# Fewer warm-up matmuls, a shorter layer norm of tile 0 and re-ordered first loads in an MLP kernel on one core

## The chip, the cores and the metric

One core of a Trainium2 chip runs the whole program. The metric is the device time of one launch in microseconds (us), the median of several launches. The time is about 1.75 us longer than the span of the trace (first to last instruction), so the two are used side by side.

## The reference

```python
B, S, D, F = 1, 2048, 1024, 3584          # all inputs bf16
def reference(x, w1, b1, w2, b2):
    y = (x - mean(x)) / sqrt(var(x) + 1e-5)          # over the last axis
    h = gelu_tanh(y @ w1 + b1)
    return h @ w2 + b2
```

## The kernel before

Both products are done as 2x2 block products with seven products in place of eight. For that the normalised and transposed tiles y are combined on VectorE into **T sums** (T1 to T4), and w1 and w2 into sums of their own. The rows of x come in tiles of 128. Tiles 0 to 3 are transposed by TensorE and multiplied at once, in small "waves". Tiles 4 to 7 are transposed by DMA, and only when they have landed can the T sums be made. What I call **the join** is the point where TensorE, done with the products that need only y (the first 60 large matmuls), goes on to those that need T sums. What I call **the head** is all that TensorE does up to its first wave.

The kernel schedules itself. Each operation is a task with an engine, an estimated duration and the data that it reads and writes. A list scheduler fixes the order on each engine; a packer then gives every buffer its place in memory by a random search from a seed, and each shared place is one more dependency. A task's latest start (`alap`) follows from its users, or from a "due" time that is given by hand.

```python
# the scheduler: among the tasks that are READY, the one with the smallest alap is started
while q and q[0][0] <= now + 1e-9:            # q: waiting tasks, by the time at which they are ready
    _, _, t = heapq.heappop(q)
    heapq.heappush(heaps[e], (t.alap, t.i, t))
...
t.alap = fin - t.lat - t.dur * 1.3 - 0.1      # fin: the users' alap, or the due time if that is earlier

# the head
for ch in range((RH + 1) // 2):
    w1_load(0, ch, "A1")                      # two loads of 256 KB each; they depend on nothing
for i in range(4):
    pr.due = (None, HEAD_LN[i]); norm(i)      # x tile -> statistics -> rstd -> y
...
for bank in range(7):
    warm(1, bank=bank, full=True)             # 128x512 matmuls of ones, to wake the clock
warm(20)                                      # 128x128
for n, c in ((8, c_st[0][0]), (8, c_mv[0]), (6, c_rstd[0])):
    warm(n, c)                                # 8 more behind each stage of tile 0's norm
to_yT_pe(0, 0, (7, 6, 5, 4))                  # tile 0 through TensorE, in four pieces
...                                           # waves of tiles 0 to 3
# the join's other arm
def to_yT_dma(b, i):                          # tiles 4 to 7
    dma("SP", lambda e: e.dma_start_transpose(dst, v16(xbuf)), ...)
def tsum(b, t):                               # four sums of one tile, 128x512 each, on DVE
    T1 = B12 - B11;  T2 = B22 - T1;  T3 = B22 - B12;  T4 = B21 - T2
for i in range(4, 8):
    due(lambda: (to_yT_dma(0, i), tsum(0, i - 4)), HEAD_DUE[0] + HEAD_DUE[1] * (i - 4))()
```

(The body of `tsum` is put in short form; "..." are cuts.)

## Time and profile before

| | kernel before |
|---|---|
| time, median (range) | 333.39 us (333.37 to 333.67, 3 runs) |
| span of the profiled execution | 332.7 us, in a launch of **334.39 us** |
| TensorE, first warm-up / clock released / first wave | 1.07 / 7.02 / 8.63 us |
| TensorE at the join / wait there / long row of matmuls from | 30.21 / 0.4 / 30.61 us |
| VectorE busy | 90% |

The timeline of the kernel before shows the other arm of the join. The columns of the timeline are the start, the busy time, engine, line and operation, then the output, the inputs, the number of instructions, and in brackets the idle time ahead and what ended it.

```profile
18.98 5.93 SPq L733 DMA_TRANSPOSE mem<-mem  x3
24.51 1.54 DVE L751 TENSOR_TENSOR mem<-mem 128x512 f16<-128x512 f16 x4
25.88 1.23 SPq L733 DMA_TRANSPOSE mem<-mem  x1
26.56 4.66 DVE L751 TENSOR_TENSOR mem<-mem 128x512 f16<-128x512 f16 x12 [0.50 <-DMA mem<-mem]
30.61 1.69 PE L920 MATMUL ps<-mem 128*128 128x512 f16 x7 [0.40 <-DVE mem L751]
```

The four transposes are issued by SP from 18.98 us on. The first lands at 24.25 us and VectorE makes its four sums. The second lands at 26.54 us.

### The profile page before, as it was taken

What the parts mean: (1) busy time and instruction counts of PE and PEld (TensorE: products, weight loads), DVE (VectorE), ACT (ScalarE), POOL (GpSimd) and SP (SyncE); (2) the same over time, 40 slices, a digit from 0 to 9 for tenths busy, and PEclk for the clock granted to TensorE, in tenths of its full rate; (3) what the DMA queues carried; (4) which work ended last, traced back from release to release, by engine and by line L of the source; (5) the groups of instructions that cost most, each with busy time, mean ns of one, the idle gap of its engine ahead of it and who ended that gap; (6) DMA issues with size and microseconds to landing.
All of it is one profiled execution on the core that took longest, in us unless ns stands there. A gap on an engine that the chain in (4) does not pass through costs nothing.

```text
span 332.7 us, 4721 instructions
## 1 busy us (share of the span) xinstructions
PE 328.1 (99%) x1692; PEld 156.2 (47%) x1692; DVE 299.3 (90%) x488; ACT 181.8 (55%) x311; POOL 13.6 (4%) x29
## 2 busy tenths in 40 slices
PE   8999999999999999999999999999999999999996
PEld 6943444444444444444444444444444444444445
DVE  4988999998999949995899999889999999989974
ACT  3796999898677676677775553561211214211411
POOL 2210013011000000000000000000000000000000
PEclk9999999999999999999999999999999999999999
DMA  7998799999998999999965464555599957999868
GB/s 214 323 226 197 241 303 311 303 267 255 311 322 266 307 367 282 307 351 352 282 189 167 150 180 120 162 165 166 128 254 240 270 194 194 244 298 278 192 132 196
DMA packets 121185, 80.73 MB, mean 243 GB/s; under 512 B 35146, under 2 KB 112586, under 8 KB 121162
## 3 DMA queue, kind: packets, MB, share of 16 engines
q1 hardware_dynamic: 118106, 79.32, 86.4%
q10 hardware_dynamic: 3056, 1.11, 1.4%
q8 instruction: 13, 0.21, 0.2%
q14 instruction: 10, 0.08, 0.1%
HBM read 48.70 MB, written 24.38 MB: 220 GB/s over the span
## 4 chain that ended last, share of the span: by engine, by line
PE 90%; SPq 5%; DMA 4%; DVE 0%; issue 0%
PE ps L920 45%; PE ps L1262 44%; SPq L774 3%; DMA mem<-mem 2%; DMA mem<-in_w_dram 1%; SPq L646 1%; PE ps L1269 1%; DVE mem L751 0%; SPq L1310 0%; PE ps L1142 0%; DVE mem L1231 0%; SPq L643 0%; SPq L1311 0%
## 5 line engine op out<-in xcount | busy, mean ns | idle before, releaser
L920 PE MATMUL ps<-mem 128*128 128x512 f16 x756 | 164.0, 379 | 0.4 <-DVE mem L751 0.4
L1262 PE MATMUL ps<-mem 128*128 128x512 f16 x672 | 145.7, 379 | 0.0
L920 PEld LDWEIGHTS ps<-mem 128*128 128x128 f16 (+1 forms) x756 | 73.5, 98 | 89.9 <-ACT mem L845 1.4
L845 ACT COPY mem<-ps 128x512 f32<-128x512 f32 x111 | 64.6, 589 | 73.5 <-PE ps L1262 59.8
L1262 PEld LDWEIGHTS ps<-mem 128*128 128x128 f16 (+1 forms) x672 | 65.7, 98 | 79.3
L829 ACT ACTIVATE mem<-ps,b_sb 128x512 f16<-128x512 f32 x112 | 73.4, 693 | 23.2 <-PE ps L920 13.8
L853 DVE TENSOR_TENSOR ps<-ps,mem 128x512 f32<-128x512 f32 x84 | 57.9, 692 | 14.3 <-ACT mem L845 12.4
L1077 DVE TENSOR_TENSOR mem<-mem 128x2048 f16<-128x2048 f16 (+1 forms) x56 | 59.6, 1083 | 1.6 <-PE ps L1262 0.8
L785 DVE TENSOR_TENSOR mem<-mem 128x1024 f16<-128x1024 bf16 (+1 forms) x56 | 37.7, 683 | 1.6 <-DMA mem<-in_w_dram 1.2
L986 DVE TENSOR_TENSOR mem<-mem 128x512 f16<-128x512 f16 (+5 forms) x84 | 36.8, 459 | 0.3
L1089 DVE TENSOR_TENSOR mem<-mem 128x2048 f16<-128x2048 f16 (+1 forms) x32 | 33.4, 1082 | 1.8 <-PE ps L1262 1.2
L836 ACT COPY ps<-ps 128x512 f32<-128x512 f32 x31 | 17.8, 574 | 23.1 <-DVE mem L1161 14.9
L671 DVE BATCH_NORM_STATS2 st_sb<-mem 128x6 f32<-128x512 bf16 x22 | 14.2, 679 | 3.6 <-DMA mem<-in_x_dram 3.6
L970 DVE TENSOR_TENSOR mem<-mem 128x2048 f16<-128x2048 bf16 (+1 forms) x16 | 17.3, 1080 | 0.1
L1161 DVE TENSOR_TENSOR mem<-ps,mem 128x512 f32<-128x512 f32 x24 | 16.3, 681 | 0.1
L1114 DVE TENSOR_TENSOR mem<-ps,mem 128x512 bf16<-128x512 f32 x22 | 14.9, 682 | 0.9 <-PE ps L1262 0.8
L751 DVE TENSOR_TENSOR mem<-mem 128x512 f16<-128x512 f16 x32 | 12.1, 419 | 1.9 <-DMA w_scr<-mem 0.9
L677 POOL TENSOR_TENSOR rstd_sb<-vpe_sb,nhalf 128x1 f32<-128x1 f32 x11 | 7.1, 647 | 54.0 <-DVE vpe_sb L674 54.0
L1293 PE MATMUL ps<-ones 128*128 128x128 bf16 (+1 forms) x55 | 7.7, 322 | 1.1 <-POOL ones L611 1.1
L1248 ACT COPY ps<-b_sb 128x512 f32<-128x512 f32 x6 | 3.5, 588 | 7.7 <-DVE mem L1161 7.6
L653 ACT ACTIVATE mem<-mem 128x1024 f16<-128x1024 bf16 x5 | 5.3, 1069 | 3.6 <-DMA mem<-in_x_dram 3.6
L1335 PE MATMUL ps<-mem 128*128 128x128 f16 x112 | 7.2, 219 | 0.0
(43 smaller groups left out, 81.0 us busy)
## 6 DMA issues: line engine op xcount, KB each, us to landing
mem<-in_w_dram SPq DMA_DIRECT2D x80, 256.0 KB, 5.0
mem<-w_scr SPq DMA_DIRECT2D x28, 448.0 KB, 4.1
w_scr<-mem SPq DMA_DIRECT2D x21, 512.0 KB, 5.3
w_raw<-mem SPq DMA_DIRECT2D x12, 512.0 KB, 5.5
mem<-w_raw SPq DMA_DIRECT2D x12, 448.0 KB, 4.3
mem<-in_w_dram SPq DMA_DIRECT2D x9, 448.0 KB, 3.7
mem<-in_x_dram SPq DMA_DIRECT2D x15, 256.0 KB, 4.3
out_dram<-mem SPq DMA_DIRECT2D x12, 256.0 KB, 4.3
```

The source lines that it names most:

```text
L785: op("DVE", d_tt(n), lambda e: e.tensor_tensor(out=o[0], in0=a[0], in1=bb[0], op=f), r=[a[1], bb[1]], w=[o[1]], name=f"w1S{k}_{ch}")
L829: op("ACT", A_GELU, lambda e: e.activation(out=dst, in_=banks[bank][:, :], func=ACT.Gelu_apprx_tanh, bias=b1_sb[:, f:f + 1], scale=1.0), r ...
L836: op("ACT", A_CP, lambda e: e.copy(out=banks[dst][:, :], in_=banks[src][:, :]), r=[bank_c[src]], w=[bank_c[dst]], name=name, lat=A_LAT)
L845: op("ACT", A_CP, lambda e: e.copy(out=v16(a, 0, 2048, F32), in_=banks[src][:, :]), r=[bank_c[src]], w=[a.c()], name=name, lat=A_LAT)
L853: op("DVE", D_PS, lambda e: e.tensor_tensor(out=banks[dst][:, :], in0=banks[src][:, :], in1=v16(a, 0, 2048, F32), op=ALU.add), r=[bank_c[s ...
L920: i = e.matmul(banks[bank][:, :], lhsT=lv[:, k, :], rhs=rv[:, k, :], start=(fresh and k == 0), stop=(k == KH - 1), skip_group_check=True)
L970: op("DVE", d_tt(2 * self.n), lambda e: e.tensor_tensor(out=vd, in0=va, in1=vb, op=ALU.subtract), r=self.cells(a) + self.cells(bb), w=self ...
L986: tt = lambda o, a, c: (lambda e: e.tensor_tensor(out=o, in0=a, in1=c, op=ALU.subtract))
L1077: op("DVE", d_tt((k1 - k0) * 512), lambda e, a=a, bb=bb, o=o: e.tensor_tensor(out=o, in0=a[0], in1=bb[0], op=f), r=a[1] + bb[1], w=[t.c(z) ...
L1089: op("DVE", d_tt((k1 - k0) * 512), lambda e, va=va, vb=vb, vd=vd: e.tensor_tensor(out=vd, in0=va, in1=vb, op=f), r=h_cells(b, a, s, k0, k1 ...
L1161: op("DVE", D_PS, lambda e: e.tensor_tensor(out=av(dst), in0=banks[bank][:, :], in1=av(src), op=ALU.add), r=[bank_c[bank], src.c()], w=[ds ...
L1262: i = e.matmul(banks[bank][:, :], lhsT=bv[:, k, :], rhs=av3[:, k, :], start=(fresh and k == 0), stop=(k == KQ - 1), skip_group_check=True)
```

## The change

The intent is to start the first real matmul earlier. Warm-ups are fewer and read a built-in constant, so they wait for no memset; they are spread over the stages of tile 0's norm. The eps of the layer norm enters as a fifth triple of the statistics (mean 0, variance eps x D), which saves an instruction between the variance and the rstd (the reciprocal of the standard deviation). First loads and due times are re-ordered, with another packing seed.

```diff
-ACT_LN = (2, 8, 10, 13, 15)
+ACT_LN = (2, 8, 11, 14)
...
-DUE_Y = 26.0
+DUE_Y = 20.0
...
-Y1_AT, Y1_STEP = -6, 6
+Y1_AT, Y1_STEP = -8,7
...
-SEED = 2
+SEED = 22
-HEAD_DUE = (4.0, 2.0)
-HEAD_LN = (4.0, 6.2, 11.1, 10.3)
-TE_DUE = 5.0
+HEAD_DUE = (2.0, 1.2)
+HEAD_LN = (4.4, 7.6, 11.1, 12.2)
+TE_DUE = 7.4
+T0_PARTS = ((7, 0, 2, "DVE", 1), (5, 2, 4, "DVE", 1), (6, 4, 8, "ACT", 1))
+W_DUE = (5.5, 9.0)
...
-        st_sb = sb("st_sb", [P, NT, 12], F32)
+        st_sb = sb("st_sb", [P, NT, 15], F32)
...
+            op("POOL", 0.1, lambda e: e.memset(st_sb[:, :, 12:14], 0.0), w=[c_ep0], name="ep0")
+            op("POOL", 0.1, lambda e: e.memset(st_sb[:, :, 14:15], LN_EPS * D), w=[c_ep1], name="ep1")
...
-                op("DVE", 0.1, lambda e: e.tensor_scalar(out=vpe_sb[:, i:i + 1], in0=mv_sb[:, i, 1:2], scalar1=LN_EPS,
-                                                          scalar2=None, op0=ALU.add),
-                   r=[c_mv[i]], w=[c_vpe[i]], name=f"eps{i}", lat=0.15)
...
-                        i = e.matmul(o, lhsT=ones[:, :], rhs=rhs, start=True, stop=True, skip_group_check=True)
+                        i = e.matmul(banks[bank][:, 0:w], lhsT=nc.const_aps.tensor(1.0, [P, P], BF16), rhs=nc.const_aps.tensor(1.0, [P, w], BF16),
+                                     start=True, stop=True, skip_group_check=True)
...
-                w1_load(0, ch, "A1")
+                w1_load(0, ch, "A1", (None, W_DUE[ch]) if ch < len(W_DUE) else None)
...
-            warm(20)
-            for n, c in ((8, c_st[0][0]), (8, c_mv[0]), (6, c_rstd[0])):
+            warm(5)
+            for n, c in ((7, c_st[0][0]), (5, c_mv[0]), (6, c_rstd[0])):
                 warm(n, c)
```

(Cut: the eps of the tiles normalised on ACT, which becomes an ACT instruction; the way tile 0's pieces are listed; the stages at which W2 is loaded; estimated durations.)

More of the change, by code (lines that the diff above doesn't have):

```diff
@@ L510 @@
 A1_LA, A2_LA, SUM_LA = (12, 12), (12, 12), (6, 7)
-ACT_LN = (2, 8, 10, 13, 15)
+ACT_LN = (2, 8, 11, 14)
 UNIT_LA, IN_LA = (6, 5, 5, 6, 7, 10, 12), 5
-W2_AT = ((0, 2, ("A", 0), ("A", 44)), (2, 4, ("A", 44), ("B", 26)), (4, 6, ("B", 26), ("B", 64)), (6, 7, ("B", 64), ("B", 78)))
+W2_AT = ((0,2,("A",0),("A",52)),(2,4,("A",52),("B",30)),(4,6,("B",30),("B",64)),(6,7,("B",64),("B",86)))
 S1_AT = -2
 W2_K = 2
-DUE_Y = 26.0
+DUE_Y = 20.0
 DUE_W = 26.0
 NACC = 5
-Y1_AT, Y1_STEP = -6, 6
+Y1_AT, Y1_STEP = -8,7
 T_PE = 6.0
-SEED = 2
-HEAD_DUE = (4.0, 2.0)
-HEAD_LN = (4.0, 6.2, 11.1, 10.3)
-TE_DUE = 5.0
-FIN_DUE, END_DUE = 12.0, 4.0
+SEED = 22
 END_ORDER = "11 10 p41 50 p40 p31 61 p30 71 60 51 70 30 31 40 41 t3 20 t7 21"
 END_HOW = {(0, 1, 0): "PE", (1, 1, 0): "PE"}
+FIN_DUE, END_DUE = 12.0, 4.0
+HEAD_DUE = (2.0, 1.2)
[3 more added lines that the diff above has]
+W_DUE = (5.5, 9.0)
 OPA = {1: "A11", 2: "A12", 3: "S4", 4: "A22", 5: "S1", 6: "S2", 7: "S3"}
@@ L585, in bass_standalone__mixer_channel_mlp__prompt_kernel @@
         NT = ST // P
-        st_sb = sb("st_sb", [P, NT, 12], F32)
+        st_sb = sb("st_sb", [P, NT, 15], F32)
+        eps_sb = sb("eps_sb", [P, 1], F32)
         mv_sb = sb("mv_sb", [P, NT, 2], F32)
@@ L619, in build @@
             op("POOL", 0.2, lambda e: e.memset(nhalf[:, :], -0.5), w=[c_nh], name="nhalf")
+            c_ep0, c_ep1, c_eps = Cell(), Cell(), Cell()
+            op("POOL", 0.1, lambda e: e.memset(st_sb[:, :, 12:14], 0.0), w=[c_ep0], name="ep0")
+            op("POOL", 0.1, lambda e: e.memset(st_sb[:, :, 14:15], LN_EPS * D), w=[c_ep1], name="ep1")
+            op("POOL", 0.1, lambda e: e.memset(eps_sb[:, :], LN_EPS), w=[c_eps], name="eps")
             op("ACT", 1.4, lambda e: e.preload_act_table(ACT.Gelu_apprx_tanh), name="table")
@@ L659, in norm @@
                     M.free(junk)
-                    eng, dur = ("DVE", 0.1) if i < 8 else ("POOL", 0.4)
-                    op(eng, dur, lambda e: e.tensor_scalar(out=vpe_sb[:, i:i + 1], in0=mv_sb[:, i, 1:2], scalar1=1.0 / D, scalar2=LN_EPS,
-                                                           op0=ALU.mult, op1=ALU.add),
-                       r=[c_st[i][0]], w=[c_vpe[i]], name=f"eps{i}", lat=0.2)
+                    if i < 8:
+                        op("ACT", 0.25, lambda e: e.activation(out=vpe_sb[:, i:i + 1], in_=mv_sb[:, i, 1:2], func=ACT.Identity, scale=1.0 / D,
+                                                               bias=eps_sb[:, :]),
+                           r=[c_st[i][0], c_eps], w=[c_vpe[i]], name=f"eps{i}", lat=A_LAT)
+                    else:
+                        op("POOL", 0.4, lambda e: e.tensor_scalar(out=vpe_sb[:, i:i + 1], in0=mv_sb[:, i, 1:2], scalar1=1.0 / D,
+                                                                  scalar2=LN_EPS, op0=ALU.mult, op1=ALU.add),
+                           r=[c_st[i][0]], w=[c_vpe[i]], name=f"eps{i}", lat=0.2)
                     op("POOL", 0.5, lambda e: e.tensor_tensor(out=rstd_sb[:, i:i + 1], in0=vpe_sb[:, i:i + 1], in1=nhalf[:, :], op=ALU.pow),
                        r=[c_vpe[i], c_nh], w=[c_rstd[i]], name=f"rstd{i}", lat=0.2)
-                    op("DVE", 0.47, lambda e: e.tensor_scalar(out=v16(b), in0=v16(b, 0, D * 2, BF16), scalar1=mv_sb[:, i, 0:1],
+                    op("DVE", 0.52, lambda e: e.tensor_scalar(out=v16(b), in0=v16(b, 0, D * 2, BF16), scalar1=mv_sb[:, i, 0:1],
                                                               scalar2=rstd_sb[:, i:i + 1], op0=ALU.add, op1=ALU.mult),
@@ L672, in norm @@
                        r=[b.c(h)], w=[c_st[i][h]], name=f"stats{i}_{h}", lat=0.1)
-                op("DVE", 0.25, lambda e: e.bn_aggr(mv_sb[:, i, :], st_sb[:, i, :]), r=c_st[i], w=[c_mv[i]], name=f"aggr{i}", lat=0.1)
-                op("DVE", 0.1, lambda e: e.tensor_scalar(out=vpe_sb[:, i:i + 1], in0=mv_sb[:, i, 1:2], scalar1=LN_EPS,
-                                                          scalar2=None, op0=ALU.add),
-                   r=[c_mv[i]], w=[c_vpe[i]], name=f"eps{i}", lat=0.15)
-                op("POOL", 0.5, lambda e: e.tensor_tensor(out=rstd_sb[:, i:i + 1], in0=vpe_sb[:, i:i + 1], in1=nhalf[:, :], op=ALU.pow),
-                   r=[c_vpe[i], c_nh], w=[c_rstd[i]], name=f"rstd{i}", lat=0.2)
+                op("DVE", 0.25, lambda e: e.bn_aggr(mv_sb[:, i, :], st_sb[:, i, :]), r=c_st[i] + [c_ep0, c_ep1], w=[c_mv[i]],
+                   name=f"aggr{i}", lat=0.15)
+                op("POOL", 0.5, lambda e: e.tensor_tensor(out=rstd_sb[:, i:i + 1], in0=mv_sb[:, i, 1:2], in1=nhalf[:, :], op=ALU.pow),
+                   r=[c_mv[i], c_nh], w=[c_rstd[i]], name=f"rstd{i}", lat=0.2)
                 for o, n in ((0, D * 2),) if i else ((0, D), (D, D)):
-                    op("DVE", 0.47 if i else 0.27, lambda e, o=o, n=n: e.tensor_scalar(
+                    op("DVE", 0.52 if i else 0.31, lambda e, o=o, n=n: e.tensor_scalar(
                         out=v16(b, o, n), in0=v16(b, o, n, BF16), scalar1=mv_sb[:, i, 0:1], scalar2=rstd_sb[:, i:i + 1],
@@ L692, in yv, with to_yT_pe @@
                 return v3(y[b, c], 0, KD * CT * 2, KD)
-            def to_yT_pe(b, i, where):
+            def to_yT_pe(b, i, parts):
                 c, t = (i % 8) // 4, i % 4
@@ L699, in to_yT_pe, with tr @@
                 yy = yv(b, c)
-                n = KD // len(where)
-                for j, bank in enumerate(where):
-                    ks = range(j * n, (j + 1) * n)
+                for bank, k0, k1, eng, pieces in parts:
                     pv = banks[bank][:, :].bitcast(F16).rearrange("p (k s) -> p k s", k=KD)
-                    def tr(e, ks=ks, pv=pv):
-                        for k in ks:
+                    def tr(e, k0=k0, k1=k1, pv=pv):
+                        for k in range(k0, k1):
                             r = e.transpose(out=pv[:, k, :], in_=v16(xbuf, k * 256, 256), identity=ident[:, :])
                         return r
-                    op("PE", n * MM128, tr, r=[xbuf.c(h) for h in sorted({k // KH for k in ks})] + [c_id], w=[bank_c[bank]],
-                       name=f"T{i}", lat=PE_LAT)
-                    m = min(n, KH)
-                    for k in range(j * n, (j + 1) * n, m):
+                    op("PE", (k1 - k0) * MM128, tr, r=[xbuf.c(h) for h in sorted({k // KH for k in range(k0, k1)})] + [c_id],
+                       w=[bank_c[bank]], name=f"T{i}", lat=PE_LAT)
+                    m = (k1 - k0) // pieces
+                    for k in range(k0, k1, m):
                         src, dst = pv[:, k:k + m, :], yy[:, k:k + m, t * P:(t + 1) * P]
                         w = [y[b, c].c((k // KH, t))] if m == KH else [y[b, c].c((k // KH, t, k))]
-                        if j % 2:
-                            op("DVE", 0.11 + m * P / 960, lambda e, src=src, dst=dst: e.tensor_copy(out=dst, in_=src),
+                        if eng == "DVE":
+                            op("DVE", 0.05 + m * P / 960, lambda e, src=src, dst=dst: e.tensor_copy(out=dst, in_=src),
                                r=[bank_c[bank]], w=w, name=f"Te{i}_{k}", lat=0.1)
@@ L720, in to_yT_pe @@
                                r=[bank_c[bank]], w=w, name=f"Te{i}_{k}", lat=A_LAT)
-                M.free(xbuf)
             def y_cells(b, c, h, t):
@@ L766, in build, with w1_load @@
             W = {}
-            def w1_load(b, ch, which):
+            def w1_load(b, ch, which, due=None):
                 i = int(which[1]) - 1
@@ L773, in w1_load @@
                     bf = W[b, ch, f"{i + 1}{h + 1}"] = M.alloc(KH * 512, f"w1{i}{h}_{b}{ch}")
+                    pr.due = due if h == 0 else None
                     dma("SP", lambda e, h=h, bf=bf: e.dma_start(v3(bf, 0, KH * 512, KH, BF16), w1v[:, h * KH:(h + 1) * KH, o:o + 256]),
                         [], [bf.c()], P * KH * 512, None, f"w1{i}{h}_{b}{ch}")
+                pr.due = None
             def w1_sums(b, ch):
@@ L1289, in f @@
                 def f(e):
+                    w = 4 * P if full else P
                     for _ in range(n):
-                        rhs = ones[:, :].rearrange("p (t c) -> p t c", t=1).to_broadcast([P, 4, P]) if full else ones[:, :]
-                        o = banks[bank][:, :].rearrange("p (t c) -> p t c", t=4) if full else banks[bank][:, 0:P]
-                        i = e.matmul(o, lhsT=ones[:, :], rhs=rhs, start=True, stop=True, skip_group_check=True)
+                        i = e.matmul(banks[bank][:, 0:w], lhsT=nc.const_aps.tensor(1.0, [P, P], BF16), rhs=nc.const_aps.tensor(1.0, [P, w], BF16),
+                                     start=True, stop=True, skip_group_check=True)
                     return i
-                op("PE", n * (MM512 if full else MM128), f, r=[c_ones] + ([gate] if gate is not None else []), w=[bank_c[bank]], name="warm")
+                op("PE", n * (MM512 if full else MM128), f, r=[gate] if gate is not None else [], w=[bank_c[bank]], name="warm")
             def due(f, after):
@@ L1319, in build @@
                 warm(1, bank=bank, full=True)
-            warm(20)
-            for n, c in ((8, c_st[0][0]), (8, c_mv[0]), (6, c_rstd[0])):
+            warm(5)
+            for n, c in ((7, c_st[0][0]), (5, c_mv[0]), (6, c_rstd[0])):
                 warm(n, c)
-            pr.due = (None, TE_DUE)
-            to_yT_pe(0, 0, (7, 6, 5, 4))
+            for part in T0_PARTS:
+                pr.due = (None, TE_DUE + (2.0 if part[1] >= KH else 0.0))
+                to_yT_pe(0, 0, (part,))
             pr.due = None
+            M.free(xb[0])
             warm(5, bank=3)
@@ L1355, in build @@
                 if t < 3:
-                    to_yT_pe(0, t + 1, (7,))
+                    to_yT_pe(0, t + 1, ((7, 0, 8, "ACT", 2),))
+                    M.free(xb[t + 1])
                 else:
```

## The prediction

> **What bounds the kernel now.** I read the page first, then the chain of waits in order of time, then the timeline of the first 32 us, because parts 1 and 2 say that nothing else can be gained.
>
> ```profile
> PE 328.1 (99%) x1692; PEld 156.2 (47%) x1692; DVE 299.3 (90%) x488; ACT 181.8 (55%) x311; POOL 13.6 (4%) x29
> ```
>
> TensorE (PE) is busy in 99% of the span. The chain shows what it does with that time and what stands ahead of it:
>
> ```profile
> 16.97 4.52 DMA mem<-in_w_dram
> 21.49 8.15 DMA mem<-mem x2
> ...
> 30.10 0.02 issue
> 30.12 0.44 DVE mem L751
> 30.56 0.05 issue
> 30.61 147.80 PE ps L920 x684
> ```
>
> From 30.61 us on it is one unbroken row of 128x512 matmuls at 147.80 / 684 = 0.216 us each; the view of waits by TensorE finds only two waits in the whole run, 1.1 us at the very start (for the memset of `ones`) and 0.4 us at 30.6. 1428 large matmuls x 0.216 = 308.4 us of the 332.7, and the diff takes none away. So the change can only act in two places: **when the first real matmul starts**, and **the join at 30.6 us**, where TensorE waits for T sums (L751, DVE) that wait for four DMA transposes of tiles 4 to 7. The chain ends before that join in transfers, not in TensorE: the head of TensorE is at present *not* what sets the end. That is the main point of this case.
>
> Now the head, in the timeline:
>
> ```profile
> 1.07 6.91 PE L1293 MATMUL ps<-ones 128*128 128x512 bf16 x49 [1.07 <-POOL ones L611]
> ...
> 4.89 0.21 DVE L673 BATCH_NORM_AGGREGATE mv_sb<-st_sb 128x2 f32<-128x12 f32 x1
> 5.14 0.15 DVE L674 TENSOR_SCALAR vpe_sb<-mv_sb 128x1 f32<-128x1 f32 x1
> 5.21 1.28 DVE L671 BATCH_NORM_STATS2 st_sb<-mem 128x6 f32<-128x512 bf16 x2
> 5.38 0.56 POOL L677 TENSOR_TENSOR rstd_sb<-vpe_sb,nhalf 128x1 f32<-128x1 f32 x1 [3.59 <-DVE vpe_sb L674]
> ...
> 6.40 0.72 DVE L680 TENSOR_SCALAR mem<-mem,mv_sb,rstd_sb 128x512 f16<-128x512 bf16 x2
> ...
> 7.82 0.61 PE L707 MATMUL ps<-ident,mem 128*128 128x128 f16 x8
> ...
> 8.63 0.83 PE L1335 MATMUL ps<-mem 128*128 128x128 f16 x12
> ```
>
> Tile 0's statistics end at 5.10, rstd at 5.94, yet its norm starts at 6.40 (DVE was inside tile 1's statistics) and its transposes at 7.82, a full us after the first half of the norm (about 6.75). What held them is the row of warm-ups: in order on the same engine, they last until 7.8. The first real matmul starts at 8.63.
>
> ```profile
> 6.00:7.00 1.00, 1.00 (x12) 1.00 (x11) 1.00 (x3) 0.90 (x1) 0.00 (x0) 1.00 1.05 324
> 7.00:8.00 1.00, 1.00 (x21) 1.00 (x19) 0.40 (x3) 0.25 (x2) 0.49 (x1) 1.00 1.17 333
> ```
>
> In these windows TensorE's instructions per us go from 12 to 21: the starts of the records are 0.107 us apart up to 7.02 us and 0.056 us after it. The warm-ups ran at half speed until then, so 42 small ones overshot.
>
> **What the Trainium skill says.** (1) "TensorE: Matmul & The Clock Gate", Part 1: the engine starts at half clock and is released after about 3.4 us of sustained work, counted in windows that run free of the kernel; starts at N = 128 are then 107 ns apart cold and 56 ns warm. The trace agrees on 107 and 56; here the release came 6.0 us after the first warm-up, so more than one window. (2) Same page, on queue depths: ScalarE and VectorE queues are strict first in, first out. The norm stuck behind tile 1's statistics agrees. (3) "DMA: Bandwidth & Descriptors", HWDGE ordering: on each engine descriptors are consumed in ring order. The landings agree: the loads of x2, x3 and the first four 256 KB w1 pieces complete at 6.08, 6.76, 7.76, 8.65, 9.55 and 10.42 us, in order of issue, about 0.87 us apart (some 300 GB/s). So a load moved ahead gains whole places of 0.7 to 0.9 us, and another loses them.
>
> **The change, part by part.**
> *Built-in constant.* The memset of the constant ones stands at 0.36 us, before the barrier; the engines are released at about 0.72. Warm-ups can start at about 0.78 in place of 1.07: 0.3 us earlier, worth that only to the clock.
> *Fewer warm-ups.* 7 large (0.427 us cold) end at 0.78 + 2.99 = 3.77. Then 5 x 0.107 to 4.30; 7 behind the first statistics (4.27) to 5.05; 5 behind the aggregation (5.10 plus about 0.05) to 5.69; 6 behind rstd. Cold sum 2.99 + 23 x 0.107 = 5.45 us against 2.99 + 42 x 0.107 = 7.48. They no longer overshoot.
> *eps as a fifth triple.* The aggregation reads 15 in place of 12 elements (0.21 us, hardly changed) and the L674 instruction goes. From the end of the aggregation (5.10) to rstd's start is 0.28 now; without the middle step about 0.09, so rstd ends at 5.94 - 0.19 = 5.75. Over 11 tiles DVE loses 11 x 0.15 = 1.7 us of work. Among tiles 8 to 15 three in place of four are now normalised on ACT, so one tile's statistics move to DVE (2 x 0.64 = +1.3 us, far from the head). Neither is on the path of the end as long as TensorE's row has no waits.
> *Tile 0.* rstd at 5.75; warm-ups to 6.44 (cold) or 6.15 (warm). The norm's first half 5.8 to 6.15, or to 6.7 if DVE again takes tile 1's statistics first. Transposes: four small ones, 0.43 us cold or 0.23 warm; then from the trace 0.2 us to the copy and two DVE copies at a pitch of 0.22 with 0.29 for the last, then 0.1 to the matmul. Best case 6.25 + 0.23 + 0.2 + 0.4 + 0.1 = about 7.2; cold 7.5; with a statistics instruction (0.64) of tile 1 in the way 7.9. I take **7.45, so 1.2 us earlier** than 8.63.
> *Loads.* The first wave needs w1's piece 0, which lands at 7.76 today. Unless it is moved ahead it would itself set the start. The new due times (5.5 and 9.0 for pieces 0 and 1, tile 3's norm moved from 10.3 to 12.2) should lift it over x3, by one place of 0.7 to 0.85 us: 7.0. Piece 1 is then at 7.9, needed 0.45 us after the wave's start, about 7.9: just about hidden.
> *The join.* The sums are now due 2.0 + 1.2 us per tile behind the waves in place of 4.0 + 2.0, so 2.0, 2.8, 3.6 and 4.4 us earlier; the transposes, which now queue behind w1 loads on SP (first issue 18.98, landings 24.25, 26.54, 27.43 and 29.64), are issued ahead of some of those. To be harmless the last must land about 1.6 us earlier, at 28.0, since TensorE would arrive at the join at 30.21 - 1.2 = 29.0. 2 to 4 us of priority should be enough.
>
> **Sum:** 1.2 us of head + 0.4 us of wait at the join = 1.6 us at best. I allow 0.3 us for a new short wait in the waves or the join: **1.3 us, 333.4 - 1.3 = 332.1 us**.
>
> **Rivals.**
> (a) *The join stays.* If the transposes don't land earlier, TensorE runs up to the same 30.6 and waits 1.6 us in place of 0.4: 333.4, nothing gained. For it: the chain today runs through transfers. Against: the due times moved by more than the head.
> (b) *The clock stays low.* With gaps between the warm-ups the release may come later; each us of half speed after 6.4 costs half a us. At a release at 8.4 in place of 7.0 some 0.5 to 0.7 us is lost: 332.7. Against: until the release the warm-ups still fill almost all of the time up to 5.7 us.
> (c) *w1 becomes the bound of the waves.* If pieces 0 to 3 land as now (7.76 to 10.42), the wave starts at 7.9 and stalls between rows: gain 0.8 in all, 332.6.
> (d) *New packing of memory* (another seed, other due times): waits on buffers in the first 60 us, where DVE is over 90% busy; up to 1 us lost, 333 to 334. In the run before none is seen after 30.6.
>
> **Range and chances.** 332.1, and 8 in 10 between 331.4 (all hidden, and a smoother wave) and 333.2 (rival a or d in part). 2% is 6.7 us, four times what the head can give: faster 0.005, same 0.985, slower 0.01.
>
> **What would show it.** TensorE's first instruction at about 0.78; no L674-like instruction behind the aggregation; the first transposes at 6.2 to 6.6; the first 12 wave matmuls at 7.2 to 7.9; the last DMA transpose landing before 28.5; no wait of TensorE at the join, and the long row of matmuls starting near 29.1. I am wrong if that row starts at 30 or later, or if TensorE has waits after it.

## The result, and the profile after

| | before | changed |
|---|---|---|
| time, median (range, runs) | 333.55 us (333.37 to 334.31, 6) | 334.0 us (333.34 to 334.56, 6) |
| ratio, changed over before | | 1.0009, 95% interval 0.9992 to 1.0027 |
| span of the profiled execution | 332.7 us | 332.8 us |

A ratio is the mean time of one kernel's fast runs over that of the other's fast runs of the same rounds, so it is not quite the ratio of the medians. The time is the same, as the class said; the 332.1 us was not reached, and 334.0 lies outside the range.

The head did what it was meant to. This is the timeline of the changed kernel:

```profile
0.83 3.58 PE L1301 MATMUL ps<-const-bfloat16-1.0 128*128 128x512 bf16 x12 [0.83 <-PEq L1596]
4.82 0.23 DVE L685 BATCH_NORM_AGGREGATE mv_sb<-st_sb 128x2 f32<-128x15 f32 x1
5.13 0.56 POOL L687 TENSOR_TENSOR rstd_sb<-mv_sb,nhalf 128x1 f32<-128x1 f32 x1 [3.24 <-DVE mv_sb L685]
6.20 0.72 PE L715 MATMUL ps<-ident,mem 128*128 128x128 f16 x8
6.38 0.68 DVE L683 BATCH_NORM_STATS2 st_sb<-mem 128x6 f32<-128x512 bf16 x1
7.24 0.42 DVE L724 COPY mem<-ps 128x256 f16<-128x256 f16 x2
7.72 0.84 PE L1346 MATMUL ps<-mem 128*128 128x128 f16 x12 [0.51 <-DVE mem L724]
```

Between the aggregation and the rstd there is no instruction any more, and rstd ends at 5.69 us in place of 5.94. Tile 0 goes to TensorE at 6.20 in place of 7.82, and the first wave starts at 7.72 in place of 8.63. It could have started sooner: a statistics instruction of tile 1 (6.38, 0.68 us) stands on VectorE ahead of the copies of tile 0 (7.24), and TensorE waits 0.51 us for them.

The profile is of a launch of 334.50 us, the second slowest of the six. What came of it is seen in the chain of waits of the changed kernel (start, length, what):

```profile
20.95 5.37 DMA mem<-mem
26.32 0.02 issue
26.34 4.19 DVE mem L758 x12
30.52 0.05 issue
30.57 147.95 PE ps L929 x684
```

and in its timeline:

```profile
16.04 13.11 PE L929 MATMUL ps<-mem 128*128 128x512 f16 x60
18.04 8.98 SPq L740 DMA_TRANSPOSE mem<-mem  x4
24.90 0.88 DVE L758 TENSOR_TENSOR mem<-mem 128x512 f16<-128x512 f16 x2 [1.03 <-DMA mem<-mem]
26.34 4.84 DVE L758 TENSOR_TENSOR mem<-mem 128x512 f16<-128x512 f16 x14 [0.56 <-DMA mem<-mem]
30.57 1.68 PE L929 MATMUL ps<-mem 128*128 128x512 f16 x7 [1.42 <-DVE mem L758]
```

TensorE is at the join at 29.15 us, 1.06 us earlier than in the profile of before, and waits there for 1.42 us. The long row starts at 30.57 us, as before (30.61), and takes as long (147.95 against 147.80 us for 684 matmuls). The transposes are issued from 18.04, only 0.94 us earlier. They land at 24.88, 26.32, 27.72 and 29.00 us, the first one later than before. VectorE makes two sums of tile 4, then idles 0.56 us with the other two undone, because in the new plan T1 of the next tile stands ahead of them. Then twelve sums in a row, 4.19 us, lie between the second landing and the end of the wait.

The view of waits by TensorE says the same in one line; its columns are what waited for what, the total, the number of waits and the longest:

```profile
PE ps L929 <- DVE mem L758: 1.4, 1, 1.4
PE ps L1346 <- DVE mem L724: 0.5, 1, 0.5
```

### The profile page after: what moved, and what is told of

Same layout as the page of the kernel before. It is cut to its first block, busy times and chain, and to the rows that moved or that the text cites. A ratio compares the mean times of both kernels' runs of the same rounds, so it can differ in the third digit from the quotient of the medians.

```text
span 332.8 us, 4669 instructions
## 1 busy us (share of the span) xinstructions
PE 326.4 (98%) x1672; PEld 153.9 (46%) x1673; DVE 299.9 (90%) x479; ACT 179.7 (54%) x307; POOL 15.2 (5%) x31
## 4 chain that ended last, share of the span: by engine, by line
PE 90%; SPq 4%; DMA 3%; DVE 1%; issue 0%
PE ps L929 45%; PE ps L1271 44%; SPq L782 3%; DMA mem<-mem 2%; DMA mem<-in_w_dram 1%; DVE mem L758 1%; SPq L653 1%; PE ps L1278 1%; SPq L1319 0%; PE ps L1151 0%; DVE mem L1240 0%; SPq L650 0%; SPq L1320 0%
## 5 line engine op out<-in xcount | busy, mean ns | idle before, releaser
L683 DVE BATCH_NORM_STATS2 st_sb<-mem 128x6 f32<-128x512 bf16 x24 | 15.3, 673 | 3.6 <-DMA mem<-in_x_dram 3.5
L687 POOL TENSOR_TENSOR rstd_sb<-mv_sb,nhalf 128x1 f32<-128x1 f32 x12 | 8.5, 711 | 45.7 <-DVE mv_sb L685 45.6
L690 DVE TENSOR_SCALAR mem<-mem,mv_sb,rstd_sb 128x1024 f16<-128x1024 bf16 (+1 forms) x13 | 6.6, 515 | 1.3 <-POOL rstd_sb L687 1.2
L1346 PEld LDWEIGHTS ps<-mem 128*128 128x128 bf16 x112 | 6.4, 98 | 1.0 <-DVE mem L724 0.7
```

## The experiments

**Theory J (the join).** The head gained, but the other arm of the join (transposes, then T sums) did not move, so TensorE only waits longer there. Then the time is the start of the long row plus a constant: 332.7 - 30.6 = 302.1 us for before, 332.8 - 30.6 = 302.2 us for the changed kernel. **Rivals:** the new packing or the changed work on VectorE costs something later on; the head is slower in most executions than in the profiled one.

"Replanned" below means that the scheduler and the packer ran anew after the edit. "Plan held" means that the plan was made as before, and then only the order of the named tasks (or only the number of warm-ups sent out) was changed; memory places and all else stay, and semaphore waits follow from the dependencies, so such a kernel is still free of races. Every kernel gave correct results.

### The changed kernel again

> The changed kernel once more, beside the next three. My theory (the join): the first wave starts near 7.7 us, TensorE then waits 1 to 1.6 us at the join for the T sums, and the long row of matmuls starts at 30.4 to 30.7 as in the kernel before, so the time is that of the kernel before within 0.6 us. Rival (the head is what counts and something later lost the gain): the long row starts near 29.2 and waits appear after it.

```profile
20.91 5.03 DMA mem<-mem
25.97 4.13 DVE mem L758 x12
30.14 147.80 PE ps L929 x684
```

This is its chain: the second transpose, twelve sums, the long row. The wait at the join was 1.12 us, and 30.14 + 302.1 = 332.2 us is the span. Time 333.83 us. The finding repeats, and the 0.4 us between the two executions is that of the second landing. (The calls ran on different devices of the same kind, so a time is best compared with the kernel before of its own call; across calls that one's median was 333.55 to 333.76 us.)

### Three replanned repairs, all of which missed

*More warm-ups, to delay the head:*

```diff
-            for n, c in ((7, c_st[0][0]), (5, c_mv[0]), (6, c_rstd[0])):
+            for n, c in ((7, c_st[0][0]), (5, c_mv[0]), (24, c_rstd[0])):
```

> The changed kernel with 18 more small warm-ups ahead of tile 0's transposes: the first wave starts 0.8 to 1.0 us later. Theory of the join: the wait at the join shrinks by the same 0.8 to 1.0 us (to about 0.4), the long row starts at 30.4 to 30.7 as before and the time is that of the changed kernel within 0.3 us. Rival (TensorE's head sets the end): 0.8 to 1.0 us slower.

The first wave started at 8.73 us, and the long row at 29.91 without a wait at the join; but a new stop of 0.54 us came at 60.8 us, where the new plan differs. 334.31 us: not clean. (The length of a stop is the time between two starts of matmuls less the usual 0.216 us; the view of waits shows somewhat less, here 0.4.)

*T1 and T2 of all four tiles ahead of T3 and T4:*

```diff
-                op("DVE", d_tt(n), tt(B12, B22, B12), r=cy(1, 1), w=cy(1, 0), name=f"T3_{b}{t}")
-                op("DVE", d_tt(n), tt(tv[4][:, :, s], B21, tv[2][:, :, s]), r=cy(0, 1) + ct(2), w=ct(4), name=f"T4_{b}{t}")
+                late34.append(...)   # for b == 0: T3, T4 are built last and depend on T2 of tile 7
```

> The changed kernel with the T1 and T2 sums of all four tiles on VectorE ahead of T3 and T4, which the first product behind the join doesn't need. Theory of the join: the last transpose still lands near 29.0, two sums of 0.44 follow, the long row starts near 29.9 in place of 30.57 and the run is 0.5 to 0.7 us faster than the changed kernel. If VectorE's order has nothing to do with it: no difference.

*The same, with the last pair of the first half's w1 loads (chunk 5) behind the norm of tile 7, so that the transposes get ahead of it:*

```diff
-            for ch in range((RH + 1) // 2):
+            for ch in range((RH + 1) // 2 - 1):     # six chunks; the last, chunk 5, comes behind norm(7) and waits for it
```

> The changed kernel with T1 and T2 first and with the two w1 loads of the last piece issued behind the four transposes in place of ahead of them. Theory of the join and its queue: the transposes land 1.5 to 1.8 us earlier (last near 27.3), no wait is left at the join, the long row starts at 29.1 to 29.3, 1.2 to 1.5 us faster than the changed kernel and the kernel before. Rival (queue order is irrelevant, transposes are slow in themselves): last landing still near 29, gain as in the run with the sums alone.

Times: 337.75 and 338.64 us, 4 and 5 us slower, where both theories expected less. The view of waits by TensorE tells why, first of the re-ordered sums:

```profile
PE ps L1278 <- DMA mem<-w_raw: 2.0, 1, 2.0
PE ps L1278 <- DVE ps L869: 1.3, 1, 1.3
PE ps L936 <- DVE mem L760: 0.6, 1, 0.6
```

then of both together:

```profile
PE ps L1280 <- DVE mem L1095: 2.8, 1, 2.8
PE ps L938 <- DMA mem<-in_w_dram: 1.1, 1, 1.1
```

The wait at the join was gone in the first of the two (only 0.6 us came a little later), but its long waits are those at 258 and 321 us, far from what was edited. In the second the transposes landed at 22.70 to 25.66 us, the first 2.2 and the last 3.3 us earlier, but TensorE waited 1.1 us for the w1 piece that had been put back, and 2.8 us at 253 us. A new plan brings a new packing, and its waits on buffers are larger than what was to be measured. So from here on the plan was held.

### Single repairs with the plan held

*18 more warm-ups behind rstd:*

```diff
-                    for _ in range(n):
+                    for _ in range(n + more):
...
-                warm(n, c)
+                warm(n, c, more=18 if n == 6 else 0)
```

> The changed kernel with 18 more small warm-ups ahead of tile 0's transposes, everything else (order on every engine, places in memory) held as it is in the changed kernel, which the earlier run of this kind did not do. Theory of the join: first wave 0.8 to 1.0 us later (8.5 to 8.8), the wait at the join shrinks from 1.1 to 1.4 us to 0.1 to 0.6, long row starts at 30.1 to 30.7, time that of the changed kernel within 0.3 us. Rival (TensorE's head sets the end): 0.8 to 1.0 us slower.

The first wave started at 8.16 us, 0.44 us later than in the changed kernel, and the time was 333.33 us: not slower, but 0.5 us faster than the changed kernel. It was run at another time.

```profile
8.16 0.84 PE L1346 MATMUL ps<-mem 128*128 128x128 f16 x12
29.34 2.97 PE L929 MATMUL ps<-mem 128*128 128x512 f16 x13
```

There is no wait at the join (no bracket in the second line). A head made worse by 0.44 us cost nothing, against the rival's 0.8 to 1.0 us. It is no clean sign for Theory J either, which expected the row at 30.1 to 30.7 us: the transposes landed earlier in this run (23.62 in place of 24.88 us), so both arms moved. I take that up below.

*T1 and T2 first, plan held:*

```diff
         pr = best
+        by = {t.name: t for t in pr.tasks}
+        for k, n in enumerate([f"T3_0{t}" for t in range(4)] + [f"T4_0{t}" for t in range(4)]):
+            by[n].start = max(by[n].start, by["T2_03"].start + 0.001 * (k + 1))
```

> The changed kernel with T1 and T2 of all tiles ahead of T3 and T4 on VectorE; all else, memory too, held. Theory: what holds the join in the changed kernel is VectorE's order, 12 sums in a row after the second transpose, not the last transpose. Then two sums follow the last landing (28.1 to 29.0), the long row starts at 29.1 to 29.95, 0.5 to 1.1 us faster than the changed kernel. If the last transpose were the bound: under 0.2 us. The waits of the second half that the earlier run of this kind had (2.2 us near 255, 1.5 us near 321) must be gone if they came from the new places in memory.

333.39 us, 0.4 us faster than the changed kernel (0.5 to 1.1 expected). The wait at the join is gone, the long row starts at 29.32 us, then stops for 0.4 us at 30.8 for a T3. The waits at 258 and 321 us of the replanned version are gone too: those were the packing's.

*The same, and the chunk 5 loads of w1 behind the second and the third transpose:*

```diff
+        by["w100_05"].start = by["Td5"].start + 0.001
+        by["w101_05"].start = by["Td6"].start + 0.001
```

> As the last, and the two w1 loads of the last piece issued between the transposes (after the second and after the third) in place of ahead of all four; memory held. Theory: transposes land 1 to 2 us earlier (first near 23, last near 27.5), VectorE's sums end before 28.7, no wait at the join, long row at 29.1 to 29.3: 1.0 to 1.4 us faster than the changed kernel and the kernel before, some 332.4 to 332.9. Danger: a w1 load now too late, a wait of up to 0.5 us near 26 or 28 instead.

333.14 us, ratio 0.9978 (0.9961 to 0.9995): faster than before by 0.2%, with an interval clear of 1. The chain now runs through TensorE and no longer through the transposes:

```profile
16.41 12.95 PE ps L929 x60
29.36 0.22 PE ps L1301
29.58 147.63 PE ps L929 x684
```

and in its timeline VectorE makes T1 and T2 of each tile as it lands, with idle time to spare, and the rest afterwards:

```profile
22.49 0.88 DVE L758 TENSOR_TENSOR mem<-mem 128x512 f16<-128x512 f16 x2
23.84 0.89 DVE L758 TENSOR_TENSOR mem<-mem 128x512 f16<-128x512 f16 x2 [0.47 <-DMA mem<-mem]
25.56 0.88 DVE L758 TENSOR_TENSOR mem<-mem 128x512 f16<-128x512 f16 x2 [0.84 <-DMA mem<-mem]
27.27 3.57 DVE L758 TENSOR_TENSOR mem<-mem 128x512 f16<-128x512 f16 x10 [0.82 <-DMA mem<-mem]
```

The time missed the 332.4 to 332.9 us that I had expected: 0.5 us were gained on the kernel before where 1.0 to 1.4 had been forecast. In this trace tile 0's statistics began 0.31 us later than in the changed kernel's (3.81 against 3.50 us), and the first wave came at 8.03 in place of 7.72.

*Only the warm-ups of the change, in the kernel before (18 fewer):*

```diff
-            warm(20)
+            warm(20, more=-18)
```

> One part of the change alone: the kernel before with 18 fewer warm-ups, all else held. Theory of the join: tile 0's transposes at about 6.9 in place of 7.8, first wave 0.6 to 0.9 us earlier, the wait at the join grows from 0.4 by as much, long row still at 30.4 to 30.8, time within 0.3 us of the kernel before. Rival (head sets the end): 0.6 to 0.9 us faster.

334.51 us, slower than both the theory and the rival had it. Tile 0 reached TensorE at 6.86 us, but the wave only started at 8.46, held by an ACT copy (0.6 us) and then by a w1 piece (0.2 us): without the new order of copies and loads the fewer warm-ups gain little. The row started at 30.16 us, and 0.7 us were lost at 94 us. The new wait there makes this run no clean measure of the head.

### More warm-ups elsewhere, the repairs in the kernel before, the seed

In the changed kernel's record of DMA packets a 16 KB instruction fetch of TensorE (the second that the trace holds, "the third" in the expectation below) lies amid the transposes, and the transposes' data stops there for 1 us or more, in some runs in two such pauses, the second ending soon after the fetch. The number of warm-ups moves that fetch. The next kernel has 6 more warm-ups ahead of the first gate and 12 more behind tile 0, to bring the fetch forward:

```diff
-            warm(5)
+            warm(5, more=6)
...
-            warm(5, bank=3)
+            warm(5, bank=3, more=12)
```

> The changed kernel with 18 more warm-ups put into places where TensorE is idle anyway (6 ahead of the wait for the first statistics, 12 behind tile 0's transposes), so the first wave stays near 7.7 us; all else held. Theory of the fetch: TensorE's third 16 KB instruction fetch comes after a fixed number of its instructions, so more warm-ups bring it forward (from 20.6 to 21.6 us in the changed kernel's traces to 20.0 to 20.7); it then overlaps the tail of the w1 loads, takes 1.2 us in place of 2 to 2.5, and the transposes have one pause in place of two: first landing near 23.5 in place of 24.9, last near 27.6, wait at the join at most 0.4 us, 0.6 to 1.0 us faster than the changed kernel. Rival (the earlier landings of the runs with 18 extra warm-ups were chance, or came from the later head): landings near 24.9 and 28 to 29, time as the changed kernel.

Stretches of 1 us: busy time of TensorE (with the number of instructions), weight loads, VectorE, ACT, POOL, then the granted clock, the DMA share and GB/s. First the changed kernel, then this one:

```profile
21.50:22.50 1.00, 1.00 (x6) 0.42 (x5) 0.89 (x3) 0.82 (x2) 0.00 (x0) 1.00 2.23 59
22.50:23.50 1.00, 1.00 (x6) 0.48 (x5) 0.97 (x2) 1.00 (x3) 0.00 (x0) 1.00 0.21 4
```

```profile
21.50:22.50 1.00, 1.00 (x6) 0.49 (x5) 0.96 (x2) 0.82 (x2) 0.00 (x0) 1.00 0.58 129
22.50:23.50 1.00, 1.00 (x7) 0.41 (x6) 0.97 (x2) 1.00 (x3) 0.00 (x0) 1.00 1.28 283
```

In the changed kernel 59 and 4 GB/s pass in these two microseconds, here 129 and 283. The first transpose landed at 23.15 us in place of 24.88, TensorE did not wait at the join, the row started at 29.09 and the span was 331.1 us. The time of 333.47 us (0.9989, interval 0.9975 to 1.0003) is on the side expected, without being clear of 1; the trace is of the fastest of the six launches (332.87 us). The fetch itself was at 19.27 us, not at the 20.0 to 20.7 I had forecast.

> The same 18 warm-ups in idle places together with T1 and T2 first and the two w1 loads between the transposes. Theory: the join had no wait left in the run with the latter two, so the fetch can give nothing more: long row at 29.1 to 29.6, set by the head alone, 332.9 to 333.3 us. If it gets clearly faster, a wait remained that I did not see.

This one joins those warm-ups with the two repairs of the run of 333.14 us: 333.41 us, ratio 1.0001 (0.9981 to 1.0021), so not clear of the kernel before. In its trace the first wave came at 8.16 us, TensorE did not wait, and the row started at 29.42.

The two repairs in the kernel **before**, with its old head:

> The kernel before with T1 and T2 first and the same two w1 loads between the transposes; its head is left as it is. Theory: TensorE arrives at the join at 30.2, so at most the 0.4 us wait goes; the wait near 94 us that the kernel before with few warm-ups had may give that back: 0 to 0.4 us faster than the kernel before, and so slower than the changed kernel with the same repair. Rival (the repair is worth 1 us whatever the head does): 0.8 to 1.0 us faster.

334.96 us, a miss that says nothing of the theory: in that plan the last transpose fell behind a load that waits for TensorE, and landed at 29.3 us. TensorE then waited twice, 0.8 us in all by the view of waits.

The changed kernel with the old seed (`SEED = 2`):

> The changed kernel with the memory packing's old seed, 2 in place of 22. The two runs in which everything was planned anew had waits of 1 to 3 us near 255 and 321 us from new places of buffers. If the seed was changed for that reason: such waits here, 1 to 4 us slower than the changed kernel. If the seed is free: the same within 0.3 us.

336.66 us. The long waits come at 166 us (1.1 us by the view of waits, for w1 sums) and at 320 us. The change needed another seed to stand still.

### The repair in before, mended, and the repairs repeated

To the two edits of the queue this adds the loads that had stood in the way: both `w110_01` and `w111_01` start behind the fourth transpose.

> The kernel before with T1 and T2 first, the two last w1 loads between the transposes and the gated A2 loads behind the fourth transpose; head untouched. Theory: TensorE arrives at the join at 30.2 and finds the sums ready, so 0.3 to 0.5 us faster than the kernel before at most (333.2 or later), less if the wait near 94 us returns; the changed kernel with its repair (f12) is 0.4 to 1.0 us faster than this. Rival (repair alone is worth the whole microsecond): as fast as f12.

333.92 us, ratio 1.0012 (0.9992 to 1.0033). No gain from the repair with the old head, although no wait was left at the join itself (row at 29.52, then a stop of 0.5 us at 31 us for a T3). The next run has the same repair of order and queue, a stop of the same size and the new head, and is 0.7 us faster (333.25 us; the ranges are 333.21 to 333.49 and 333.32 to 335.56): the theory's 0.4 to 1.0, and not the rival's nothing.

> The same file as f4, once more: 332.9 to 333.4 us with a narrow spread (0.4 us), ratio to the kernel before 0.997 to 0.999, no wait of TensorE at the join.

The kernel of the best run once more: 333.25 us, ratio 0.9984 (0.9972 to 0.9996). It repeats; a stop of 0.5 us at 30.6 us for a T3 is left.

> The changed kernel with 18 warm-ups in idle places and T1 and T2 first, the queue's order as in the changed kernel. Theory: last transpose near 26.5 to 28, two sums follow, no wait at the join: long row at 29.1 to 29.5 in most runs, 332.8 to 333.3 us, spread under 0.6 us. If the fetch plays no part, as the run with T1 and T2 first alone (333.4, spread 1 us).

The warm-ups in the gaps with T1 and T2 first, but with the queue left as it is: 333.18 us, ratio 0.9983 (0.997 to 0.9997), with a spread of 0.9 us where less than 0.6 was expected. TensorE has no wait at all behind its first instruction in this trace, and the span is 331.4 us.

### The kernel before, looked at three times more

One thing did not add up. If the join alone set the time of the kernel before, its repair should have paid there; and both traces of such variants (the two with the old head) had the first wave at 8.08 and 8.09 us, not 8.63. So I looked at the unchanged kernel before again.

> The kernel before, unchanged, traced again, because its profile on record belongs to an execution of 334.39 us, 0.8 to 1.0 us over its median of 333.4 to 333.8. Theory (that profile shows a late release of the clock, and is not the usual case): most of three new traces have the release near 6 us in place of 7.04, the first wave at 8.0 to 8.2 in place of 8.63, TensorE at the join by about 29.7 and the long row at 29.7 to 29.9, span 331.7 to 332.0. Rival (the head is always at 8.6 and the timed runs are faster for something later): wave at 8.5 to 8.7 in all three and row not before 30.2, so span 332.3 or more.

> As the look ahead of it: the theory expects the first wave at 8.0 to 8.2 and the span at 331.7 to 332.0 in at least two of the three; the rival the wave at 8.5 to 8.7 in all.

> As the two looks ahead of it: the theory expects the first wave at 8.0 to 8.2 and the span at 331.7 to 332.0 in at least two of the three; the rival the wave at 8.5 to 8.7 in all.

Neither theory was right as I had put it. The timelines of the three, warm-ups, first wave and the row behind the join of each:

```profile
1.07 6.92 PE L1293 MATMUL ps<-ones 128*128 128x512 bf16 x49 [1.07 <-POOL ones L611]
8.65 0.83 PE L1335 MATMUL ps<-mem 128*128 128x128 f16 x12
30.22 2.12 PE L920 MATMUL ps<-mem 128*128 128x512 f16 x9
```

```profile
1.07 6.77 PE L1293 MATMUL ps<-ones 128*128 128x512 bf16 x49 [1.07 <-POOL ones L611]
8.49 0.83 PE L1335 MATMUL ps<-mem 128*128 128x128 f16 x12
29.91 2.32 PE L920 MATMUL ps<-mem 128*128 128x512 f16 x10
```

```profile
1.07 5.96 PE L1293 MATMUL ps<-ones 128*128 128x512 bf16 x49 [1.07 <-POOL ones L611]
7.78 0.83 PE L1335 MATMUL ps<-mem 128*128 128x128 f16 x12
29.52 2.75 PE L920 MATMUL ps<-mem 128*128 128x512 f16 x12
```

The same 49 warm-ups took 6.92, 6.77 and 5.96 us, and the first wave came at 8.65, 8.49 and 7.78 us. There is no bracket in any of the last lines: **in three of four executions the kernel before does not wait at the join.** Its head sets its end there, and the head varies by 0.9 us with the moment at which the clock is released. (Add the 302.1 us of Theory J to the three rows' starts, and the spans come out: 332.3, 332.0 and 331.6 us.)

| trace | clock released | first wave | TensorE at the join | wait | long row | span |
|---|---|---|---|---|---|---|
| before, the profile | 7.0 | 8.63 | 30.21 | 0.4 | 30.61 | 332.7 |
| before, first look | 7.0 | 8.65 | 30.22 | 0 | 30.22 | 332.3 |
| before, second look | 6.8 | 8.49 | 29.91 | 0 | 29.91 | 332.0 |
| before, third look | 5.1 | 7.78 | 29.52 | 0 | 29.52 | 331.6 |
| changed | 4.2 | 7.72 | 29.15 | 1.42 | 30.57 | 332.8 |
| changed, again | 4.5 to 4.8 | 7.69 | 29.02 | 1.12 | 30.14 | 332.2 |

The means: before is at the join at 29.97 us and starts the row at 30.07; the changed kernel is there at 29.09 and starts it at 30.36. So in these traces 0.9 us was gained ahead of the join, and 1.2 us more was waited at it (1.27 against 0.1). The two traces of the changed kernel are of launches of 334.50 and 333.93 us; its fastest, 333.34 us with a span of 331.6 us, has no trace, and by the constant of 302.1 us its row would have begun near 29.5 us, with hardly a wait (an estimate).

More traces hold one of the two heads unaltered. In two further traces with the old head the first wave came at 8.08 and 8.09 us, so the mean of six is 8.29 us. With the new head it came at 7.63 to 8.03 us in eight traces (the changed kernel twice, the two replanned re-orderings, T1 and T2 first, both repairs twice, the old seed), 7.79 in the mean: 0.5 us earlier, and the profiled 7.72 is no exception. In all eight it came 4.21 to 4.22 us after VectorE's first statistics instruction, whether the clock was released at 4.2 us or only after 6.5. In the old head it moved with the release (7.78 us at 5.1, 8.49 at 6.8, 8.63 at 7.0). So in these traces the new head follows the first statistics, and no longer the clock.

### All times

| kernel | time, us (range) | before | ratio (95% interval) |
|---|---|---|---|
| changed, again | 333.83 (333.64 to 334.67) | 333.69 | 1.0003 (0.9982 to 1.0024) |
| + 18 warm-ups, replanned | 334.31 (333.95 to 334.72) | 333.69 | 1.0014 (0.9994 to 1.0034) |
| + T1, T2 first, replanned | 337.75 (336.81 to 341.39) | 333.69 | 1.0135 (1.0097 to 1.0174) |
| + T1, T2 first and queue, replanned | 338.64 (337.82 to 340.27) | 333.69 | 1.015 (1.0123 to 1.0177) |
| + 18 warm-ups, plan held | 333.33 (333.12 to 333.75) | 333.62 | 0.9986 (0.9968 to 1.0003) |
| + T1, T2 first, plan held | 333.39 (333.02 to 333.99) | 333.62 | 0.9987 (0.9969 to 1.0005) |
| + T1, T2 first and queue, plan held | 333.14 (332.99 to 333.31) | 333.62 | 0.9978 (0.9961 to 0.9995) |
| the same, repeated | 333.25 (333.21 to 333.49) | 333.76 | 0.9984 (0.9972 to 0.9996) |
| + warm-ups in gaps | 333.47 (332.87 to 333.92) | 333.67 | 0.9989 (0.9975 to 1.0003) |
| + warm-ups in gaps, T1, T2 first and queue | 333.41 (332.99 to 335.01) | 333.67 | 1.0001 (0.9981 to 1.0021) |
| + warm-ups in gaps and T1, T2 first | 333.18 (332.87 to 333.78) | 333.76 | 0.9983 (0.997 to 0.9997) |
| changed, old seed | 336.66 (336.39 to 338.53) | 333.67 | 1.0095 (1.0076 to 1.0114) |
| before with 18 fewer warm-ups | 334.51 (334.05 to 336.29) | 333.62 | 1.0025 (1.0 to 1.0051) |
| before with both repairs, first try | 334.96 (334.2 to 335.95) | 333.67 | 1.0037 (1.002 to 1.0055) |
| before with both repairs, mended | 333.92 (333.32 to 335.56) | 333.76 | 1.0012 (0.9992 to 1.0033) |
| before, three looks | 334.04, 333.69, 333.30 | 333.24 | |

All of them count as the same at 2%. Within that, three runs of versions with both the new head and a mended join are 0.5 to 0.6 us faster than before, with intervals just clear of 1 (0.9978, 0.9984, 0.9983). A fourth such version, with both repairs and the warm-ups in gaps, is not (1.0001), nor are the changed kernels with T1 and T2 first alone (0.9987) or with warm-ups alone (0.9986, 0.9989), nor the new head or the repair alone.

**What stays open.** Why the data of the transposes pauses once or twice. Fetches that started by 20.0 us went with a single pause and an early first landing (19.27 us in one run, 19.74 and 19.86 in the second and the third look at before), and at 20.64, 20.72 and 21.23 us with the long one (the changed kernel, the first look, the changed kernel again). But the run with 18 more warm-ups had its fetch at 20.66 us and one pause, and the profile of before had its fetch at 21.26 us with a first landing 5.3 us after the issue, as early as in the looks with a fetch before 20.0 (5.1 and 5.7; 6.8 in the changed kernel). That the fetch causes the pause is argued, not shown.

## Why the prediction was wrong

*Right.* Warm-ups from 0.83 us (predicted 0.78); no eps instruction; rstd at 5.69 us (5.75); tile 0 to TensorE at 6.20 (6.2 to 6.6); the first wave at 7.72, in the range of 7.2 to 7.9 and late for the reason named for 7.9, a statistics instruction of tile 1 ahead of the copies; w1 pieces 0 and 1 at 7.03 and 7.88 us (7.0 and 7.9; so close by luck, since the second trace has 6.73 and 7.57); TensorE at the join at 29.15 us (29.0); no waits that count behind the join. The class, too: the same.

*The step that failed first: "2 to 4 us of priority should be enough".* The due times of the T sums moved by 2.0 to 4.4 us, and the first transpose by 0.94 us between the two profiles; over all traces of the two kernels it moved by 0.2 us in the mean (18.41 to 18.19), and the last landing by 0.35 us (28.88 to 28.53). The same fourteen w1 pieces stand ahead of the first transpose in the queue as before. The reason I read from the code: the scheduler compares due times only among tasks that are ready, the w1 loads depend on nothing and are ready from the start, and a transpose is ready only when its tile is normalised. That the queue held it, and not the tile, is shown: tile 4 was normalised at 16.00 us and its transpose issued at 18.04, and with the two last of the fourteen loads out of the way it was issued at 16.15 us. The condition I had set, a last landing by 28.0 us, was not met (29.00; 28.06 in the second trace). Rival (a), "the join stays", is what happened, and it had been given as 333.4 us.

*A term missing from the sum.* I asked only when the last transpose lands. What the wait ends with is VectorE: twelve sums, 4.19 us, behind the second landing. The new due times made this a little worse, since T1 of the next tile now stands ahead of T3 and T4 of the one that has landed. So "0.3 us for a new short wait" measured 1.42 and 1.12 us.

*A term mis-sized: "so 1.2 us earlier than 8.63", taken off 333.4.* The 8.63 us come from a launch of 334.39 us, and I took the gain off a median of 333.39. Over four traces of before the wave starts at 8.39 us in the mean, and as early as 7.78; over all traces with either head the gain is 0.5 us (8.29 to 7.79). The "0.4 us of wait at the join" was there in one trace of four. And the sentence that the head "is at present *not* what sets the end" held for that trace alone: in the other three it did set it.

So even with the join mended the sum was too large: the three clear mended runs came to 333.14 to 333.25 us against 333.62 to 333.76, a gain of about 0.5 us where 1.3 was predicted.

*Half right: rival (d).* The new packing did no harm in the changed kernel, because the seed was changed with it; with the old seed it cost 2.7 us.

## What to carry to other kernels

Where two arms meet, shortening one moves the wait to the other: work out when the other arm would be ready, down to its last instruction on each engine, before counting a gain. In a list scheduler like this one a due time does not move a task past others that were ready and queued long before it; a dependency or a fixed order did. A profile is one execution: compare its own time with the median before a gain read from it is taken off that median, and test small edits with the plan held, since another packing seed alone cost the changed kernel 2.7 us.

## What the Trainium skill lacked or had wrong

- "TensorE: Matmul & The Clock Gate", Part 1, "What you observe", puts the release at around 4 us of sustained matmuls, give or take 500 ns from run to run. In four traces of the same kernel, all with the first warm-up at 1.07 us, it came 4.0, 5.7, 6.0 and 6.0 us after it: a spread of 1.9 us, which moved the first wave by 0.87 us.
- "DMA: Bandwidth & Descriptors", "DMA Transpose (X-bar)", gives constraints, but not the time from issue to landing of a transpose that is queued behind loads, and no word that its data can pause. Here a transpose of a 256 KB tile landed 4.4 us after its issue in the median, four of them kept the issuing queue busy for 8.98 us, and their data fell to 59 and 4 GB/s in two successive microseconds of one run and stayed at 129 and 283 in another.
- "Runtime: NRT & Kernel Launch", "Instruction fetch mechanics", has blocks of 16 KiB (256 instructions) and a cost that is mostly hidden. The count agrees (13 fetches of 16 KB for the 3345 matmuls and weight loads recorded of the changed kernel, about 257 each). It gives no duration: the fetch amid the transposes took 0.97 to 2.5 us in these traces.
